# Loading wq, wk and wv four rows to a partition, in an attention and MLP layer on one core

## The chip, the cores and the metric

The kernel runs on one core of one Trainium2 chip. The metric is the device time of one execution in microseconds, as the median of several runs. A run's profile has a span of its own, from the first instruction of the program to the last; the device time is a little longer. The engines are named as the profile names them: PE (TensorE, matrix products; PEld its weight loads), DVE (VectorE), ACT (ScalarE), POOL (GpSimd) and SP (SyncE, which here only issues DMAs).

## The reference

The input x has 2048 rows of 576 values. It is normalised, projected by wq, wk and wv (576 x 576 each), and goes through attention with 32 heads of 18 values in four segments of 512 rows. Each segment attends causally to itself and adds a gated look-up in a memory that the segments before it have built. Then come wo, a residual sum, a second normalisation, and an MLP with 4608 hidden values and gelu.

```
x = A_x
h = x + _A_ref(_layernorm(x, axis=-1), A_wq, A_wk, A_wv, A_wo, A_beta)
h2 = h + _B_ref(_layernorm(h, axis=-1), B_w1, B_b1, B_w2, B_b2)

# in _A_ref, B, S, D, H = 1, 2048, 576, 32
q = (x @ wq)...; k = (x @ wk)...; v = (x @ wv)...        # reshaped to 32 heads, 4 segments
logits = jnp.einsum('bhqd,bhkd->bhqk', qs, ks) * scale + mask
a_dot = jnp.einsum('bhqk,bhkd->bhqd', _softmax(logits, axis=-1), vs)
num = jnp.einsum('bhld,bhde->bhle', pq, M)
den = jnp.einsum('bhld,bhd->bhl', pq, z)[..., None] + 1e-06
o = g * num / den + (1.0 - g) * a_dot
M = M + jnp.einsum('bhld,bhle->bhde', pk, vs)
z = z + jnp.einsum('bhld->bhd', pk)
return o @ wo

# in _B_ref
h = _gelu(jnp.einsum('bsd,df->bsf', x, w1) + b1)
return jnp.einsum('bsf,fd->bsd', h, w2) + b2
```

All inputs are bf16. What matters for this change is the product x @ w over 576 terms: a sum over rows of w, and in whatever order the rows are taken, it is the same sum as long as the values of x are taken in the same order.

## The kernel before

**Tiles.** The 2048 rows are 16 tiles of 128 rows; two tiles make one of 8 chunks of 256 rows. A projection contracts over 576 = 4 x 128 + 64 rows of a weight. So a tile of x, normalised, is turned by PE or by a DMA into `xT`, five blocks of 128 columns; the fifth block holds the last 64 columns of x twice, in its lower and its upper 64 partitions (`again`, lines 398 and 399, writes the second copy). A projection is four matmuls over 128 partitions (`mm4`, line 352) and a tail over 64.

**The tail has two forms.** Whole (`mm_last`, line 356): one matmul over 128 partitions, whose other 64 rows in the weight are zeros (`wpad_q` and the like). Paired (`Part.tail`, line 447): two tails of two column ranges run side by side, one on the lower and one on the upper 64 rows of PE. The set `WHOLE` says which pairs are done as whole tails. `Half.tail` (line 765) is the same for w1.

**The weights of the projections.** `wqkv` has 128 partitions by five blocks by 3 x 576 columns. Block k holds rows 128 k to 128 k + 127, one row to a partition. wq and wk come in two loads each, of 432 and of 144 columns (`wqkv` and `wqkvr`), wv in one; the 64 rows of the tails come in five more. The columns of the projections are cut in parts: 432 of q, 432 of k, 432 of v, and the remaining 144 of each. The first two tiles project the remaining columns of q and k together (288), and those of v alone (144).

**The first normalisation** (`layernorm`). DVE takes the statistics of x, two `BN_STATS` and one `BN_AGGR`. For tiles 0 and 1 it subtracts the mean only (line 381), and the scale, which POOL works out beside it, is multiplied in when the projections leave PSUM (line 519 on ACT, 517 on DVE). For the others ACT (line 394) or DVE (line 387) does both. x of a tile is loaded into one of four buffers, `x_p` and `x_b`.

**The order.** Every piece of work is an `Op` with a number, the engine, and what it reads and writes. Tables of numbers fix the rest: `ORDER` is the sequence in which all are issued, so each engine's own sequence too; `FLIP` lists the ops that run on their second engine (DVE or ACT, DVE or POOL); `PLACE` gives each PSUM result one of eight banks. Every engine works through its own sequence strictly in order, and SP issues all DMAs from one such sequence. At the start PE multiplies zeros 17 times (`zeros`, line 335) while the first tile of x is on its way, and ACT, DVE and POOL fill buffers with zeros.

**Scores and values.** A score group (line 638) is 16 matmuls on 32 rows of PE, four at a time; ACT takes the exponential of 128 x 2048 results (line 642); POOL sets the part above the diagonal to zero (line 646); a value group (line 654) is 16 matmuls, four at a time on 32 columns each. The MLP's matmuls (lines 352 and 872) stand between these. The weights w1 come in pieces of 512 columns through a few buffers, w2 stays in SBUF.

Of the kernel before, what the change touches and what calls it, by code (L numbers as in the profile page):

```python
# [9 lines left out]
ALU = mybir.AluOpType  # L10
# [6 lines left out]
def kernel(  # L17
# [49 lines left out]
    def sbuf(name, shape, dt=BF16):  # L67
        return sb.tile([P] + shape, dt, name=name)

    PLACE = {  # L70
# [35 lines left out]
    }  # L106
    WHOLE = {
        246, 379, 406, 469, 470, 542, 543, 852, 853, 1174, 1175, 1286, 1500, 1501, 2141, 2142,
    }

    class Op:
# [980 lines left out]
```

## Time and profile before

| | |
|---|---|
| Median of 3 runs | 451.72 us (451.48 to 451.95) |
| The profiled execution | 452.2 us, span 450.5 us |
| PE busy | 443.6 us of the span |
| ACT busy | 331.1 us |
| DVE busy | 270.6 us |
| POOL busy | 230.5 us |
| Granted PE clock, mean of the span | 0.999 |

PE is busy nearly throughout, and the granted clock is full. Matmuls overlap in the pipeline, and a matmul's row gives the time from its start to its end, not the time by which it holds up the next; that is read from the starts of neighbouring rows. A row of the timeline has the start, the duration and the count of instructions that stand together; a bracket names what the engine waited for. A row of the waits has the total, the count and the longest.

### The profile page before, as it was taken

To read this page: it belongs to the slowest core of one execution; us is meant where nothing else is said; L and a number is where in the kernel's file an instruction comes from. 1 tells how busy PE (TensorE), PEld (TensorE's weight loads), DVE (VectorE), ACT (ScalarE), POOL (GpSimd) and SP (SyncE) were. 2 spreads that over 40 slices of the span, in tenths; PEclk is the share of its full clock that TensorE was granted. 3 is DMA by queue.
4 is the path that set the end of the run, shared out by engine and by line. 5 is a ranking of instruction groups with operands and counts; after the bars stand their busy time and mean duration, and the time that the engine had idled before them with its cause. 6 is when DMAs were issued, how large, how long until landed. Compare 5 with 4: busy or idle time off the path is not lost.

```text
span 450.5 us, 14512 instructions
## 1 busy us (share of the span) xinstructions
PE 443.6 (98%) x6090; PEld 333.5 (74%) x6090; DVE 270.6 (60%) x620; ACT 331.1 (73%) x313; POOL 230.5 (51%) x416
## 2 busy tenths in 40 slices
PE   7999999999999999999999999999999999999997
PEld 4556977676777777676777677777878888888886
DVE  7899998877797567577648665657352534212111
ACT  8899999998978966979779877687876544241740
POOL 6888956798975387646546865653240203000000
PEclk9999999999999999999999999999999999999999
DMA  7799879979699559796673686586666655474411
GB/s 191 214 205 233 203 192 317 191 140 160 179 197 192 168 134 190 210 166 171 140 175 109 169 183 181 167 209 169 202 180 161 202 169 157 132 224 144 140 41 52
DMA packets 114353, 78.40 MB, mean 174 GB/s; under 512 B 48832, under 2 KB 112240, under 8 KB 114288
## 3 DMA queue, kind: packets, MB, share of 16 engines
q1 hardware_dynamic: 114288, 77.48, 68.5%
q8 instruction: 47, 0.77, 0.8%
q14 instruction: 18, 0.15, 0.1%
HBM read 60.09 MB, written 7.08 MB: 149 GB/s over the span
## 4 chain that ended last, share of the span: by engine, by line
PE 94%; DMA 3%; SPq 2%; DVE 1%; issue 0%; DVEq 0%
PE bank L352 29%; PE bank L872 24%; PE st L352 9%; PE st L872 7%; PE st L638 6%; PE bank L654 5%; PE bank L698 3%; PE bank L765 3%; PE bank L356 2%; DMA w1g<-in_B_w_dram 1%; PE st L698 1%; DMA wqkv<-in_A_wq_dram 1%; PE st L765 1%; PE bank L546 1%; PE bank L608 1%; PE bank L447 1%
## 5 line engine op out<-in xcount | busy, mean ns | idle before, releaser
L642 ACT ACTIVATE pt<-st 128x2048 bf16<-128x2048 f32 x80 | 150.1, 1877 | 39.0 <-PE st L638 31.2
L872 PEld LDWEIGHTS <-hT 128*128 128x128 bf16 x1188 | 110.4, 98 | 28.9 <-issue 1.9
L872 PE MATMUL bank<-w_sb,hT 128*128 128x288 bf16 x900 | 128.9, 286 | 0.0
L352 PEld LDWEIGHTS <-w1g 128*128 128x128 bf16 x944 | 87.6, 98 | 16.3 <-issue 3.8
L646 POOL TENSOR_SCALAR_AFFINE_SELECT pt<-pt 128x512 bf16<-128x512 bf16 x128 | 79.9, 639 | 22.6 <-ACT pt L642 22.0
L352 PE MATMUL bank<-xn2T,w1g 128*128 128x256 bf16 (+1 forms) x728 | 90.8, 268 | 0.0
L786 DVE TENSOR_TENSOR hT<-bank,b1T 128x512 bf16<-128x512 f32 x77 | 51.7, 684 | 42.3 <-PE bank L352 20.8
L807 ACT ACTIVATE hT<-hT 128x1536 bf16<-128x1536 bf16 (+4 forms) x25 | 66.2, 2663 | 7.7 <-DVE hT L786 7.4
L352 PE MATMUL bank<-wqkv,xT 128*128 128x432 bf16 (+1 forms) x216 | 45.5, 342 | 1.1 <-DMA wqkv<-in_A_wq_dram 0.7
L352 PEld LDWEIGHTS <-xT 128*128 128x128 bf16 x264 | 24.6, 98 | 18.1 <-issue 1.4
L603 POOL TENSOR_TENSOR pq<-ek,pq 128x512 bf16<-128x512 bf16 x24 | 27.7, 1154 | 18.9 <-DVE ek L602 14.4
L784 ACT ACTIVATE hT<-bank,b1T 128x256 bf16<-128x256 f32 x54 | 22.1, 471 | 20.1 <-PE bank L765 14.2
L872 PE MATMUL st<-w_sb,hT 128*128 128x288 bf16 (+1 forms) x288 | 35.7, 271 | 0.0
L786 DVE TENSOR_TENSOR hT<-st,b1T 128x512 bf16<-128x512 f32 x24 | 16.4, 687 | 29.9 <-PE st L352 20.2
L784 ACT ACTIVATE hT<-st,b1T 128x256 bf16<-128x256 f32 x32 | 13.3, 474 | 26.2 <-PE st L352 21.3
L638 PE MATMUL st<-QT,KT 32*128 32x128 bf16 x1280 | 32.1, 217 | 0.0
L638 PEld LDWEIGHTS <-KT 32*128 32x128 bf16 x1280 | 18.4, 92 | 15.1 <-issue 11.5
L878 DVE TENSOR_TENSOR ot<-bank,hc 128x288 bf16<-128x288 f32 x25 | 11.2, 447 | 30.6 <-PE bank L872 20.0
L352 PE MATMUL st<-xn2T,w1g 128*128 128x256 bf16 x216 | 29.5, 273 | 0.0
L669 DVE STREAM_TRANSPOSE bank<-bank 128x512 f32<-128x512 f32 x32 | 23.1, 724 | 10.0 <-PE bank L654 9.0
L672 POOL TENSOR_TENSOR r<-r,omg 128x16 f32<-128x16 f32 x32 | 7.2, 226 | 34.9 <-DVE r L670 34.6
L654 PE MATMUL bank<-pt,v_aug 128*19 128x128 bf16 x1280 | 23.8, 220 | 0.0
(162 smaller groups left out, 655.6 us busy)
## 6 DMA issues: line engine op xcount, KB each, us to landing
w1g<-in_B_w_dram SPq DMA_DIRECT2D x57, 512.0 KB, 4.3
w_sb<-in_B_w_dram SPq DMA_DIRECT2D x12, 432.0 KB, 5.5
wqkv<-in_B_w_dram SPq DMA_DIRECT2D x10, 512.0 KB, 3.6
hd<-h_t SPq DMA_DIRECT2D x16, 288.0 KB, 3.5
hc<-hd SPq DMA_DIRECT2D x32, 144.0 KB, 2.7
w1g<-in_B_w_dram SPq DMA_DIRECT2D x114, 32.0 KB, 3.4
x_b<-in_A_x_dram SPq DMA_DIRECT2D x18, 144.0 KB, 3.9
hT<-in_B_w_dram SPq DMA_DIRECT2D x5, 512.0 KB, 4.2
```

The costliest lines, as they stand in the source:

```text
L352: nc.tensor.matmul(out=acc, lhsT=lhsT_of(slice(0, P), k), rhs=rhs_of(slice(0, P), k), start=start and k == 0, stop=False, skip_group_check ...
L603: op(("m_add", n), "POOL", lambda: nc.gpsimd.tensor_tensor(out=pq[:], in0=e_g, in1=pq[:], op=ALU.add), ["ek"], ["pq"])
L638: nc.tensor.matmul(out=st4[:, i, n * P:(n + 1) * P], lhsT=KTs[(2 * s0 + kt) % NK][rows, g, :], rhs=QTs[(2 * c + qt) % NQ][rows, g, :], sta ...
L642: op(("exp", v), "ACT", lambda pt=pt: nc.scalar.activation(out=pt[:], in_=open_four("scores")[:], func=ACT.Exp, scale=scale), [st], [("pt" ...
L646: op(("mask", v), "POOL", lambda n=n, pt=pt: nc.gpsimd.affine_select(out=pt[:, :, n * P:(n + 1) * P], in_=pt[:, :, n * P:(n + 1) * P], pat ...
L654: nc.tensor.matmul(out=bank(ox)[32 * i:32 * i + E, (g % 4) * P:(g % 4) * P + P], lhsT=v_augs[(2 * s0 + kt) % NV][:, G * i + g, :], rhs=pt[ ...
L669: op(("f_T", n), "DVE", lambda: nc.vector.transpose(out=bank(ox), in_=bank(ox)), [], [ox])
L698: nc.tensor.matmul(out=bank(b)[:, 0:HALF], lhsT=xTt[:, k, :], rhs=wo_t[:, k, hs], start=(k == 0), stop=(k == KT - 1))
L784: nc.scalar.activation(out=dst[:, j, :], in_=acc()[:, j, :], func=ACT.Identity, bias=b1T[:, j0 + j:j0 + j + 1], scale=1.0)
L786: return op(name, "DVE", lambda: nc.vector.tensor_tensor(out=dst, in0=acc(), in1=bias, op=ALU.add), [tok, "b1T"], keys, alt=("ACT", by_act ...
L807: op(("gelu", c, f0, f), "ACT", lambda: nc.scalar.activation(out=hT[:, f0:f, :], in_=hT[:, f0:f, :], func=ACT.Gelu_apprx_tanh), [], [("hT" ...
L872: nc.tensor.matmul(out=bank(b)[:, 0:w], lhsT=hT[:, q, tl * P:(tl + 1) * P], rhs=w2_sb[:, q, hs], start=(q == 0), stop=(q == NF - 1))
```

## The change

Partition p now holds rows 4 p to 4 p + 3 of each weight, one behind the other, for the first 512 rows: each partition's part is one run of 4 x 576 values, 4608 bytes, in memory and in SBUF. wq, wk and wv are one load each; the parts of 432 and 144 columns are gone, so a projection now needs the whole of each weight that it reads. The tails keep their five loads. `wqkv` is laid out as three blocks of 4 x 576 and a block of tails behind them.

So that the sums stay the same, block k of the normalised x must hold columns k, k + 4, k + 8 and so on. The normalisation does that as it writes: it reads columns four apart for the first 512. The last 64 columns and their second copy are written by an instruction of its own (`again`), which normalises x twice into 128 columns, on DVE or POOL, where before a copy of 64 columns was made from the normalised tile. It now reads x and its statistics, and no longer waits for the normalisation; the next load of x into the buffer waits for both.

`PLACE`, `FLIP`, `WHOLE` and `ORDER` are new.

```diff
-    wqkv = sbuf("wqkv", [KT, 3 * D])
+    wqkv = sbuf("wqkv", [KT * 3 * D])
+    w_main = wqkv[:, 0:12 * D].rearrange("p (t k n) -> p t k n", t=3, k=4)
+    w_tail = wqkv[:, 12 * D:15 * D].rearrange("p (t n) -> p t n", t=3)
...
     for j, W in enumerate((A_wq, A_wk, A_wv)):
-        for name, lo, hi in (("wqkv", 0, CH), ("wqkvr", CH, D)) if j < 2 else (("wqkv", 0, D),):
-            dma((name, j), hi - lo, 32, lambda j=j, W=W, lo=lo, hi=hi: nc.sync.dma_start(
-                out=wqkv[:, 0:4, j * D + lo:j * D + hi], in_=W[0:512, lo:hi].rearrange("(k p) n -> p k n", p=P)), (), [(name, j)])
+        dma(("wqkv", j), 4 * P * D * 2 / 1024, 8, lambda j=j, W=W: nc.sync.dma_start(
+            out=w_main[:, j], in_=W[0:512, :].rearrange("(p k) n -> p k n", k=4)), (), [("wqkv", j)])
...
+        first = who[0] == "p"
+        parts = [(dst[:, 0:D], src)]
+        if first:
+
+            parts = [(dst[:, 0:512].rearrange("p (k c) -> p k c", k=4), src[:, 0:512].rearrange("p (c k) -> p k c", k=4))]
+            last = (dst[:, 512:XW].rearrange("p (a c) -> p a c", a=2), src[:, 512:D].unsqueeze(1).to_broadcast([P, 2, 64]))
...
+        def normal(engine, o, i):
+            if early:
+                engine.tensor_scalar(out=o, in0=i, scalar1=mv[:, 0:1], scalar2=None, op0=ALU.subtract)
+            else:
+                engine.tensor_scalar(out=o, in0=i, scalar1=mv[:, 0:1], scalar2=rstd[:], op0=ALU.subtract, op1=ALU.mult)
+
         def by_dve():
-            nc.vector.tensor_scalar(out=dst[:, 0:D], in0=src, scalar1=mv[:, 0:1], scalar2=rstd[:], op0=ALU.subtract, op1=ALU.mult)
+            normal(nc.vector, *parts[0])
...
-            op(("apply" + name, t), "ACT", lambda: nc.scalar.activation(out=dst[:, 0:D], in_=src, func=ACT.Identity, bias=nmr[:], scale=rstd[:]),
+            op(("apply" + name, t), "ACT", lambda: nc.scalar.activation(out=parts[0][0], in_=parts[0][1], func=ACT.Identity, bias=nmr[:], scale=rstd[:]),
                [sk, skey], [(*dkey, 0)], alt=("DVE", by_dve))
...
-        op(("again" + name, t), "DVE", lambda: nc.vector.tensor_copy(out=dst[:, D:XW], in_=dst[:, D - 64:D]), [(*dkey, 0)], [(*dkey, 1)],
-           alt=("POOL", lambda: nc.gpsimd.tensor_copy(out=dst[:, D:XW], in_=dst[:, D - 64:D])))
+        if first:
+            op(("again" + name, t), "DVE", lambda: normal(nc.vector, *last), [sk, skey], [(*dkey, 1)], alt=("POOL", lambda: normal(nc.gpsimd, *last)))
...
         def cols(self, r, k):
-            w = wqkv[r, k, :].rearrange("p (t n) -> p t n", t=3)
+            w = w_main[r, :, k, :] if k < 4 else w_tail[r]
...
-        mains = {0: [("wqkv", 0)], 1: [("wqkv", 1)], 2: [("wqkvr", 0), ("wqkvr", 1), ("wqkv", 2)], 3: [("wqkv", 2)],
-                 4: [("wqkvr", 0), ("wqkvr", 1)], 5: [("wqkv", 2)]}[ch]
+        mains = [("wqkv", j) for j in js]
...
     ORDER = [
-        57, 15, 33, 26, 36, 29, 23, 0, 28, 25, 1, 67, 125, 6, 68, 58, 55, 69, 126, 70, 71, 127, 22, 27, 128, 14, 59,
```

SP's sequence at the start, before. The names are the buffer and the input; `wqkv` by 128x4x144 and 128x4x432 are the two parts of wk and wq, 64 rows are a tail:

```order
L265 DMA x_p_76<-in_A_x_dram 128x576
L265 DMA x_p_77<-in_A_x_dram 128x576
L275 DMA wqkv<-in_A_wk_dram 128x4x144
L283 DMA beta_bc<-in_A_beta_dram 128x32
L279 DMA wqkv<-in_A_wq_dram 64x576
L275 DMA wqkv<-in_A_wq_dram 128x4x144
L279 DMA wqkv<-in_A_wk_dram 64x144
L275 DMA wqkv<-in_A_wk_dram 128x4x432
L279 DMA wqkv<-in_A_wk_dram 64x432
L265 DMA x_b_78<-in_A_x_dram 128x576
L275 DMA wqkv<-in_A_wq_dram 128x4x432
L265 DMA x_b_79<-in_A_x_dram 128x576
```

And now:

```order
L268 DMA x_p_76<-in_A_x_dram 128x576
L268 DMA x_p_77<-in_A_x_dram 128x576
L280 DMA wqkv<-in_A_wk_dram 64x432
L268 DMA x_b_78<-in_A_x_dram 128x576
L276 DMA wqkv<-in_A_wk_dram 128x2304
L284 DMA beta_bc<-in_A_beta_dram 128x32
L276 DMA wqkv<-in_A_wq_dram 128x2304
L280 DMA wqkv<-in_A_wq_dram 64x576
L280 DMA wqkv<-in_A_wk_dram 64x144
L292 DMA hT_126<-in_B_b_dram 36x128
L268 DMA x_b_79<-in_A_x_dram 128x576
L276 DMA wqkv<-in_A_wv_dram 128x2304
```

The larger part of wk stood eighth and is now in the fifth load, that of wq stood eleventh and is now in the seventh. Tile 2 of x (`x_b_78`) moved from tenth to fourth.

DVE's sequence from the statistics of tile 0 on, before (`xn1_0` and `xn1_1` are the normalised tiles 0 and 1, `xT0` and `xT1` their transposes):

```order
L367 BN_STATS stats_p0_129<-x_p0_76 128x6 x2
L368 BN_AGGR mv_p0_130<-stats_p0_129 128x2
L381 TENSOR_SCALAR xn1_0_80<-x_p0_76,mv_p0_130 128x576
L261 MEMSET MZacc_74 18x8
L398 COPY xn1_0_80<-xn1_0_80 128x64
L367 BN_STATS stats_p1_133<-x_p1_77 128x6 x2
L368 BN_AGGR mv_p1_134<-stats_p1_133 128x2
L381 TENSOR_SCALAR xn1_1_81<-x_p1_77,mv_p1_134 128x576
L398 COPY xn1_1_81<-xn1_1_81 128x64
L414 COPY xT0_84<-st0_221 128x640
L339 TENSOR_SCALAR g_bc_71<-g_bc_71 128x32
L340 RECIPROCAL g_bc_71<-g_bc_71 128x32
```

And now:

```order
L369 BN_AGGR mv_p0_130<-stats_p0_129 128x2
L392 TENSOR_SCALAR xn1_0_80<-x_p0_76,mv_p0_130 128x128
L392 TENSOR_SCALAR xn1_0_80<-x_p0_76,mv_p0_130 128x512
L264 MEMSET gmz_73 128x8
L368 BN_STATS stats_p1_133<-x_p1_77 128x6 x2
L369 BN_AGGR mv_p1_134<-stats_p1_133 128x2
L392 TENSOR_SCALAR xn1_1_81<-x_p1_77,mv_p1_134 128x512
L264 MEMSET wqkv_62 64x2x72
L264 MEMSET wqkv_62 64x216
L340 TENSOR_SCALAR g_bc_71<-g_bc_71 128x32
L341 RECIPROCAL g_bc_71<-g_bc_71 128x32
L425 COPY xT1_85<-st0_206 128x640
```

The copy of the last 64 columns became a normalisation of 128, ahead of the one of 512; for tile 1 it moved to POOL. The copy of tile 0's transpose left DVE for ACT, and tile 1's came to DVE from there. Both transposes are now written to one PSUM bank, `st0`; before, tile 1's went to another.

More of the change, by code (lines that the diff above doesn't have):

```diff
@@ L213 @@
     W0 = (NCH - 2) * NG
-    done_w = wqkv[:].rearrange("p k n -> p (k n)")
+    done_w = wqkv[:]
     w1_late = [done_w[:, j * W1W:(j + 1) * W1W].rearrange("p (k f) -> p k f", f=512) for j in range(3)]
@@ L279 @@
                 dma(("wqkvt", j, r), (hi - lo) / 8, 4, lambda lo=lo, hi=hi, r=r, j=j, W=W: nc.sync.dma_start(
-                    out=wqkv[r:r + 64, 4, lo:hi], in_=W[512:576, lo - j * D:hi - j * D]), (), [("wqkvt", j, r)])
+                    out=w_tail[r:r + 64, j, lo - j * D:hi - j * D], in_=W[512:576, lo - j * D:hi - j * D]), (), [("wqkvt", j, r)])
     for tl in range(2):
@@ L459, in wkeys_of @@
         tails = [("wqkvt", j, 64 if ch in (1, 3) else 0) for j in js]
-        mains = {0: [("wqkv", 0)], 1: [("wqkv", 1)], 2: [("wqkvr", 0), ("wqkvr", 1), ("wqkv", 2)], 3: [("wqkv", 2)],
-                 4: [("wqkvr", 0), ("wqkvr", 1)], 5: [("wqkv", 2)]}[ch]
+        mains = [("wqkv", j) for j in js]
         return mains + tails + pads
-    WALL = [("wqkv", j) for j in range(3)] + [("wqkvr", j) for j in range(2)] + [("wqkvt", 0, 0)] + [
+    WALL = [("wqkv", j) for j in range(3)] + [("wqkvt", 0, 0)] + [
         ("wqkvt", j, r) for j in (1, 2) for r in (0, 64)] + ["wpad_q", "wpad_k", "wpad_t", "wpad_v"]
```

21 lines of the change are left out of this document (10 added, 11 removed), and 337 rows, old and new, of tables (FLIP, ORDER, PLACE).

## The prediction

> **What bounds the kernel now.** I read the page first, then the waits of PE, then the chain and the timeline of the first 16 us, then the two groups of DMA rows.
>
> ```profile
> PE 443.6 (98%) x6090; PEld 333.5 (74%) x6090; DVE 270.6 (60%) x620; ACT 331.1 (73%) x313; POOL 230.5 (51%) x416
> ...
> PE 94%; DMA 3%; SPq 2%; DVE 1%; issue 0%; DVEq 0%
> ```
> ```profile
> PE bank L335 <- DVE pq L294: 2.4, 1, 2.4
> PE bank L352 <- DMA wqkv<-in_A_wq_dram: 0.7, 1, 0.7
> PE st L765 <- DMA w1g<-in_B_w_dram: 0.5, 1, 0.5
> PE bank L352 <- DMA wqkv<-in_A_wk_dram: 0.2, 1, 0.2
> ```
>
> PE is the bound: 94% of the chain, and after its first instruction all of its listed waits together are 1.4 us. Time can therefore come only from less work on PE, fewer changes between its forms of matmul, or a shorter start. The start is where the loads of wq and wk stand, 0.9 us of those 1.4. Its timeline (start, duration, engine, line; the releaser in brackets), with the two rows of the chain and of the DMA list that belong to it:
>
> ```profile
> 2.73 0.56 SPq L279 DMA_DIRECT2D wqkv<-in_A_wq_dram  x1
> 3.03 0.82 DVE L367 BATCH_NORM_STATS2 stats_p<-x_p 128x6 f32<-128x288 bf16 x2
> 3.31 1.39 ACT L310 COPY hT<-pq 64x256 bf16<-64x256 bf16 x3
> 3.96 0.52 SPq L279 DMA_DIRECT2D wqkv<-in_A_wk_dram  x1
> 4.51 0.59 SPq L275 DMA_DIRECT2D wqkv<-in_A_wk_dram  x1
> 5.57 0.74 PE L411 MATMUL st<-ident,xn 128*128 128x128 bf16 x5
> 5.71 0.58 SPq L265 DMA_DIRECT2D x_b<-in_A_x_dram  x1
> 6.33 0.43 SPq L275 DMA_DIRECT2D wqkv<-in_A_wq_dram  x1
> 7.07 0.69 ACT L415 COPY xT<-bank 128x640 bf16<-128x640 bf16 x1
> 9.24 0.82 DVE L367 BATCH_NORM_STATS2 stats_p<-x_b 128x6 f32<-128x288 bf16 x2 [0.60 <-DMA x_b<-in_A_x_dram]
> ```
> ```profile
> 7.09 0.65 PE L352 MATMUL st<-wqkv,xT 128*128 128x288 bf16 x4
> ...
> 8.80 0.89 PE L352 MATMUL bank<-wqkv,xT 128*128 128x432 bf16 x4 [0.20 <-DMA wqkv<-in_A_wk_dram]
> 9.53 0.35 PE L356 MATMUL bank<-wqkv,xT 128*128 128x432 bf16 x1
> 9.71 0.89 PE L352 MATMUL bank<-wqkv,xT 128*128 128x432 bf16 x4
> ...
> 11.97 0.89 PE L352 MATMUL bank<-wqkv,xT 128*128 128x432 bf16 x4 [0.74 <-DMA wqkv<-in_A_wq_dram]
> ...
> 15.13 0.44 PE L411 MATMUL bank<-ident,xn 128*128 128x128 bf16 x5
> 15.51 0.40 PE L638 MATMUL st<-QT,KT 32*128 32x128 bf16 x16
> 15.84 0.91 PE L352 MATMUL bank<-wqkv,xT 128*128 128x432 bf16 x4
> ```
> ```profile
> 6.33 5.60 DMA wqkv<-in_A_wq_dram
> ```
> ```profile
> wqkv<-in_A_wk_dram SPq DMA_DIRECT2D x1, 432.0 KB, 4.2
> ```
>
> Read them so: x tile 0 is there at 3.03, its first projection starts at 7.09, the projection to k waits for wk at 8.80, the one to q for wq (issued at 6.33, 5.60 us on the way) at 11.97, and the first score stands at 15.51. From 8.80 to 9.53 four matmuls of 432 columns start, so one is 0.18 us; five are 0.90, and five of 288 columns 0.61 at the same rate. From 15.13 to 15.84 lie five transposes (5 x 128 columns, 0.27), 16 score matmuls that run four at a time (0.21), and 0.23 of nothing: a change of form in and one out, 0.12 each.
>
> **The change part by part.**
>
> *Loads.* SP issues about one DMA per 0.5 to 0.6 us, so a place in its order is a time. wk is now fifth (the fifth issue stood at 2.73), wq seventh (3.96), the load of x tile 3 eleventh (6.33). How long a load in pieces of 4608 bytes takes, no row shows. The bounds are the two loads of 432 KB, 4.2 and 5.6 us. I take 4.2 for wk, from the load that was also issued early, with little in front of it, although this one has a third more bytes: wk lands at 6.9. For wq the two rows give 8.2 to 9.6. The rate of the DMA engines by stretch of time (the last two columns are their busy share and GB/s):
>
> ```profile
> 4.00:6.00 2.00, 2.00 (x13) 1.49 (x12) 1.87 (x8) 1.98 (x6) 1.26 (x4) 1.00 0.69 135
> 10.00:12.00 2.00, 1.26 (x14) 0.75 (x12) 1.71 (x7) 1.27 (x3) 1.28 (x4) 1.00 1.04 331
> ```
>
> The low rate stands where the parts of 144 columns, pieces of 288 bytes, were on their way; the high one where pieces of 864 and 1152 bytes were. The Trainium skill (DMA: Bandwidth & Descriptors, Specifications) has 512 bytes as the least transfer for full rate. By that rule the parts of 144 columns gain, and 4608 bytes are no faster than 864: the load of wk would then take 4.2 x 576 / 432 = 5.6 us, and the sum below would be that of the second rival and not mine. The two rows agree with the rule below 512 bytes; above it they say nothing.
>
> *Normalisation of x.* The first 512 columns are now read four apart, and columns 512 to 575 are normalised twice by an instruction of their own in place of a copy:
>
> ```profile
> L381 DVE TENSOR_SCALAR xn<-x_p,mv_p 128x576 bf16<-128x576 bf16 x2 | 0.7, 370 | 0.1
> ...
> L724 DVE TENSOR_SCALAR xn<-h_t,mv_b,rstd_b 128x576 bf16<-128x576 f32 x8 | 4.7, 603 | 1.0 <-POOL rstd_b L719 1.0
> L561 DVE TENSOR_SCALAR ek<-ek 128x576 bf16<-128x576 bf16 x12 | 4.4, 368 | 1.8 <-ACT ek L559 1.8
> L549 DVE COPY QT<-bank 128x1024 bf16<-128x1024 bf16 x6 | 4.1, 676 | 1.3 <-PE bank L546 1.3
> ```
>
> A read four apart has no row. Bounds for 512 columns are 0.33 (the bf16 rate, 370 x 512 / 576) and 0.54 (the slowest row of this operation, 603); I take 0.5. Tile 0 is then ready at 3.03 + 0.82 + 0.2 + 0.2 + 0.5, about 4.8 to 5.0. PE is busy with the eleven multiplications by zero until 5.57, as before, so this costs nothing; without that cover it would cost up to 0.2. In the other 14 tiles, ten of them by ACT, it runs several tiles ahead of PE.
>
> *The start walked through.* The 17 multiplications by zero stay. The copy of tile 0's transpose moves from DVE to ACT, where eight zeroing copies stand ahead of it; three took 1.39 with starts 0.31 apart, all eight some 3.4, so ACT is free by 5.8, before the transpose ends at 6.3, and the copy (0.69) ends at 7.0. Tile 1's transpose now goes to the same bank and waits for that, so the first projection starts at 7.35, not at 7.09. wk (6.9) is there. k of tile 0 runs to 8.25, k of tile 1 to 9.25 (0.1 behind tile 1's copy on DVE), q of tile 0 to 10.15, the 288 columns to 10.75, q of tile 1 to 11.65, without a wait for a load unless wq is at its upper bound (0.3). The transposes of q and k of tile 0 wait for DVE, which evacuates q behind the statistics of x tile 3. That load took 3.5 in the row of x_b above (5.71 to 9.24), so it lands at 9.85, and q is out by 11.85. Two groups of eight transposes (0.43 each), the 288 columns of tile 1, two times 144 columns, five transposes: PE is done with these at about 14.3. The copies that the score needs end on DVE at 11.85 + 1.0 (four small operations) + 0.37 (L561) + 2 x 0.68 (L549) = 14.6. So the first score stands at 14.6 and not at 15.51: 0.9 earlier. Ahead of it 16 transposes fewer have been done (0.85) and ten matmuls of 144 columns more (0.6), 0.25 less work. The start is worth **-0.65 us**; bounds -1.0 and, with the rows' other ends, +0.35.
>
> *Fewer whole tails.* Counted in the two orders, the fifth matmul of a projection over the full 432 columns and 128 rows stands 24 times in place of 32, and pairs of half-row tails 19 times in place of 15. A pair runs side by side:
>
> ```profile
> 184.33 0.36 PE L447 MATMUL st<-wqkv,xT 64*128 64x432 bf16 x2
> 184.52 0.34 PE L447 MATMUL bank<-wqkv,xT 64*128 64x432 bf16 x2
> 184.70 0.27 PE L765 MATMUL st<-xn2T,w1g 64*128 64x256 bf16 x1
> 185.44 0.39 PE L765 MATMUL st<-xn2T,w1g 64*128 64x256 bf16 x3 [0.47 <-DMA w1g<-in_B_w_dram]
> ```
>
> Two pairs from 184.33 to 184.70, 0.18 each. So -8 x 0.18 + 4 x 0.18 = **-0.72**. All other matmuls have the same count and columns.
>
> *Changes of form.* Between full, half-row, score and value matmuls the order before changes 257 times, the new one 262 times: 5 x 0.12 = **+0.60**.
>
> *Stalls behind the start.* The one of before is in the last two rows: 0.47 us for a load of a w1 tail. It may go, and another may come; the new order has as many loads and moves them all. I take **0**, bounds -0.5 (none) and +2.
>
> Sum: -0.65 - 0.72 + 0.60 = -0.77. The profiled execution took 452.2 (span 450.5, 1.7 around it), 0.5 above the median of 451.72; nothing changes around the span. From the median: 450.95, and I say **450.9**. About 0.2% (0.9 us) is what a measurement of this kernel can tell from no change.
>
> **The rivals.**
>
> *No stall at all:* the new order loses the 0.47 and brings none. For it: PE's waits are down to that one; against: its loads pass the same single queue. 450.9 - 0.5 = 450.4.
>
> *Long pieces are no faster:* wk takes 5.6 us, lands at 8.3, and the first projection starts 1.0 later. The start is then worth -0.65 + 1.0 = +0.35, and the time is 451.72 + 0.35 - 0.72 + 0.60 = 451.95. For it: the second 432 KB load took just that. Against: that load had five others beside it. This is what the rule on 512 bytes in the Trainium skill (DMA: Bandwidth & Descriptors, Specifications) would make of it.
>
> *SP's queue held up by GpSimd, slower:* a buffer of x was free when its normalisation had read it; now the instruction for the last 64 columns reads it too, in 13 of 16 tiles on GpSimd. The next load of x waits for that in SP's queue, and the loads of w1 stand behind it.
>
> ```profile
> SPq L265 <- DVE xn L387: 4.7, 2, 3.8
> ...
> 179.46 0.47 SPq L744 DMA_DIRECT2D w1g<-in_B_w_dram  x1
> ```
> ```profile
> L706 POOL TENSOR_TENSOR h_t<-h_t,b_bc 128x576 f32<-128x576 f32 x16 | 20.5, 1279 | 1.9 <-DVE xn L724 1.2 <-ACT xn L729 0.6
> ```
>
> SP waits at such loads already, once for 3.8 us. The w1 tail issued at 179.46, 5.2 us before its use at 184.70, was late by 0.47, so w1 has nothing to spare there, and each further delay counts in full. Two operations of the size of L706 ahead on GpSimd are 2.5 us: 450.9 + 2.5 = 453.4. It decides from about 1.7 us on, where it has eaten the 0.77 and 0.9 more. Against: GpSimd is busy half of the span, and the order lets x be loaded a chunk ahead.
>
> **How the numbers follow.** My case has a chance of 0.48 and a spread of some 0.8 us about 450.9, as the unknown stalls and the walk make it: just over half of it is faster by more than 0.2%, the rest within. No stall at all: 0.16, faster. Long pieces no faster: 0.13, nearly all within 0.2%. SP held up: 0.23, nearly all slower. That makes 0.42 faster, 0.36 within, 0.22 slower. The range reaches from 449.7 (no stall, and the start at its better bound) to 453.2, which leaves out the worst of SP's case and a little below: under 2 in 10. My own case alone is 450.1 to 451.7.
>
> **What the profile of the changed kernel would show.** Right: no wait of PE for wqkv; the first projection near 7.35 and the first score near 14.6; 24 whole fifth matmuls and 38 tails of 432 columns; the loads of wk and wq landing by 6.9 and 9.6; the normalisation near 0.5 us on DVE. Wrong: a wait for wk or wq in PE's list (long pieces), DVE waiting for x tile 3 until after 11, waits of SP at the loads of x for GpSimd with waits of PE for w1g of 0.5 us or more behind them, or a sum of PE's waits after its first instruction above 2 us.

## The result, and the profile after

The changed kernel takes 453.44 us (median of 11 runs, 452.30 to 454.48), the kernel before 451.95 beside it (11 runs, 451.11 to 452.54). The ratio is 1.0034, with a 95% interval of 1.0022 to 1.0046: slower by about 1.5 us, where 0.8 us faster was forecast, and just above the range. The profiled execution took 453.44, its span is 451.7 (before: 452.2 and 450.5).

The page after: busy times, and the chain that ended last.

```profile
PE 444.1 (98%) x6090; PEld 332.7 (74%) x6090; DVE 274.0 (61%) x623; ACT 329.3 (73%) x311; POOL 236.9 (52%) x416
...
PE 91%; POOL 3%; DMA 2%; DVE 1%; ACT 1%; SPq 1%; issue 0%; POOLq 0%
```

The waits of PE after (for what, us in total, times, longest):

```profile
PE bank L336 <- DVE pq L295: 2.5, 1, 2.5
PE st L353 <- DVE xT L425: 1.3, 1, 1.3
PE bank L353 <- DMA xT<-xn: 0.4, 1, 0.4
PE bank L664 <- issue: 0.2, 1, 0.2
PE bank L353 <- DMA wqkv<-in_A_wk_dram: 0.2, 1, 0.2
```

The wait for wq and the one for a w1 tail are gone. In their place stands one of 1.3 us for a copy on DVE, and two small ones near 36 and 53. The chain of the changed kernel, in its first 17 us, tells who made the copy late:

```profile
3.41 5.26 DMA beta_bc<-in_A_beta_dram
...
8.70 0.24 ACT g_bc L339
...
8.96 0.19 DVE g_bc L340
...
9.17 0.35 DVE g_bc L341
9.53 0.36 DVE xT L425
...
9.93 0.58 PE st L353 x3
```

And its timeline (start, duration, engine, line; the releaser in brackets):

```profile
3.41 0.43 SPq L284 DMA_DIRECT2D beta_bc<-in_A_beta_dram  x1
3.89 0.43 SPq L276 DMA_DIRECT2D wqkv<-in_A_wq_dram  x1
...
7.53 0.89 PE L353 MATMUL bank<-wqkv,xT 128*128 128x432 bf16 x4 [0.18 <-DMA wqkv<-in_A_wk_dram]
...
8.70 0.23 ACT L339 ACTIVATE g_bc<-beta_bc 128x32 f32<-128x32 bf16 x1 [1.84 <-DMA beta_bc<-in_A_beta_dram]
...
9.44 0.43 DVE L425 COPY xT<-st 128x640 bf16<-128x640 bf16 x1
...
9.93 0.90 PE L353 MATMUL st<-wqkv,xT 128*128 128x432 bf16 x4 [1.33 <-DVE xT L425]
...
11.55 0.82 DVE L368 BATCH_NORM_STATS2 stats_p<-x_b 128x6 f32<-128x288 bf16 x2 [0.27 <-DMA x_b<-in_A_x_dram]
...
16.02 0.40 PE L648 MATMUL st<-QT,KT 32*128 32x128 bf16 x16
```

The load of beta, 8 KB for the gate, is issued right behind wk and is on its way for 5.3 us (before: 2.7). ACT waits 1.84 for it with the exponential, DVE waits for ACT with the addition and the reciprocal of the gate, and the copy of tile 1's transposed x stands behind those two on DVE. So k of tile 1 starts at 9.93 and the first score at 16.02, 0.51 after the 15.51 of before. With the 0.25 us less work ahead of it, the start cost 0.76 where it was to bring 0.65. The last matmul starts 1.3 later than before (448.69 and 447.38), so 0.55 came behind the start.

Each profile is one execution. Three pairs of the kernels below have the same loads and instructions up to the first score, and it stood at 16.02 and 15.90, at 14.94 and 15.65, and at 15.42 and 14.64 in them. So a start that is read from one profile is uncertain by up to 0.8 us. With beta's load behind wk and ahead of wq, four kernels with the new rows and order have it at 15.9 to 16.4; with this load third, on a queue of its own or left out, five have it at 14.6 to 15.7.

### The profile page after: what moved, and what is told of

Same layout as the page of the kernel before. It is cut to its first block, busy times and chain, and to the rows that moved or that the text cites. A ratio compares the mean times of both kernels' runs of the same rounds, so it can differ in the third digit from the quotient of the medians.

```text
span 451.7 us, 14511 instructions
## 1 busy us (share of the span) xinstructions
PE 444.1 (98%) x6090; PEld 332.7 (74%) x6090; DVE 274.0 (61%) x623; ACT 329.3 (73%) x311; POOL 236.9 (52%) x416
## 4 chain that ended last, share of the span: by engine, by line
PE 91%; POOL 3%; DMA 2%; DVE 1%; ACT 1%; SPq 1%; issue 0%; POOLq 0%
PE bank L353 27%; PE bank L882 25%; PE st L353 10%; PE st L882 6%; PE st L648 5%; PE bank L664 5%; PE bank L708 3%; PE bank L775 3%; POOL pt L656 1%; PE st L775 1%; DMA beta_bc<-in_A_beta_dram 1%; PE bank L357 1%; PE bank L618 1%; DMA xT<-xn 1%; PE st L708 1%; PE bank L458 1%
## 5 line engine op out<-in xcount | busy, mean ns | idle before, releaser
L882 PE MATMUL bank<-w_sb,hT 128*128 128x288 bf16 (+1 forms) x936 | 131.2, 284 | 0.0
L353 PEld LDWEIGHTS <-w1g 128*128 128x128 bf16 x944 | 87.5, 98 | 16.4 <-issue 3.4
L353 PE MATMUL bank<-xn2T,w1g 128*128 128x256 bf16 (+1 forms) x696 | 86.2, 268 | 0.0
L796 DVE TENSOR_TENSOR hT<-bank,b1T 128x512 bf16<-128x512 f32 x75 | 50.7, 684 | 47.9 <-PE bank L353 35.8
L353 PE MATMUL bank<-wqkv,xT 128*128 128x432 bf16 (+2 forms) x212 | 43.7, 341 | 0.6 <-DMA xT<-xn 0.4
L353 PEld LDWEIGHTS <-xT 128*128 128x128 bf16 x264 | 23.6, 98 | 20.3 <-issue 1.9
L882 PE MATMUL st<-w_sb,hT 128*128 128x288 bf16 (+1 forms) x252 | 33.6, 277 | 0.0
L353 PE MATMUL st<-xn2T,w1g 128*128 128x256 bf16 x248 | 33.6, 273 | 0.0
L794 ACT ACTIVATE hT<-bank,b1T 128x256 bf16<-128x256 f32 x56 | 23.2, 473 | 13.4 <-PE bank L353 9.5
L888 DVE TENSOR_TENSOR ot<-bank,hc 128x288 bf16<-128x288 f32 (+1 forms) x26 | 11.6, 447 | 32.0 <-PE bank L882 30.7
L664 PEld LDWEIGHTS <-v_aug 128*19 128x19 bf16 x1280 | 18.2, 91 | 6.4 <-issue 3.7
```

The source lines that it names most:

```text
L353: nc.tensor.matmul(out=acc, lhsT=lhsT_of(slice(0, P), k), rhs=rhs_of(slice(0, P), k), start=start and k == 0, stop=False, skip_group_check ...
L664: nc.tensor.matmul(out=bank(ox)[32 * i:32 * i + E, (g % 4) * P:(g % 4) * P + P], lhsT=v_augs[(2 * s0 + kt) % NV][:, G * i + g, :], rhs=pt[ ...
L794: nc.scalar.activation(out=dst[:, j, :], in_=acc()[:, j, :], func=ACT.Identity, bias=b1T[:, j0 + j:j0 + j + 1], scale=1.0)
L796: return op(name, "DVE", lambda: nc.vector.tensor_tensor(out=dst, in0=acc(), in1=bias, op=ALU.add), [tok, "b1T"], keys, alt=("ACT", by_act ...
L882: nc.tensor.matmul(out=bank(b)[:, 0:w], lhsT=hT[:, q, tl * P:(tl + 1) * P], rhs=w2_sb[:, q, hs], start=(q == 0), stop=(q == NF - 1))
```

## Experiments

Each ratio is to the kernel before, in runs on the same chip, with its 95% interval. One thousandth is 0.45 us. The difference of two such ratios is uncertain by about 0.0017, or 0.8 us, where both intervals are as wide as that of the changed kernel (the two half-widths added as squares).

**The copy ahead of the gate.** Only DVE's order is changed:

```diff
 DVE:
-  g_add, g_rec,
   copy of tile 1's xT,
+  g_add, g_rec,
   statistics of x tile 2
```

> The changed kernel with two small operations on DVE, the addition and the reciprocal of the gate (g_add, g_rec), moved behind the copy of tile 1's transposed x; no load moves. Theory A, the start was lost because these two wait for the exponential of beta, whose load lands at 8.7, and the copy of tile 1 stands behind them: the copy starts near 7.4 in place of 9.44, k of tile 1 at 8.45 in place of 9.93, and the time falls by most of that 1.3 us, to 452.1 to 452.7. Rival B, the next thing in the start takes the stall over (the evacuation of q of tile 0 stands on DVE behind the statistics of x tile 3, whose load lands at 11.5): the first score moves from 16.02 to no better than 15.4, PE waits at the transposes of q instead, and the time falls by 0.6 at most, 452.8 to 453.4.

Measured: 452.88, ratio 1.0025 (1.0015 to 1.0036). Its waits of PE:

```profile
PE bank L353 <- DMA wqkv<-in_A_wq_dram: 1.8, 1, 1.8
PE bank L353 <- DMA xT<-xn: 0.5, 1, 0.5
```

k of tile 1 started at 8.37, and then PE stood for wq until 11.24: 7.3 us from issue to use. The first score stood at 16.41, not earlier than in the changed kernel, and the two ratios are too close to be told apart. B was right that something takes the stall over, but wrong on what: a load was late beneath it, in a place where the forecast had 8.2 to 9.6.

**beta third in SP's queue.**

```diff
 SP: x_p 0, x_p 1,
+    beta,
     wk tail, x_p 2, wk,
-    beta,
     wq, ...
```

> The changed kernel with the load of beta moved from sixth to third place in SP's queue, ahead of the long loads; nothing else. If its 5.3 us on the way are the company of the long pieces, it now lands in 2.7, near 4.5, g_add and g_rec are done before tile 1 is transposed, k of tile 1 starts near 8.8 (the load of wk is issued 0.4 later and lands near 7.9), and the time falls by about 0.9, to 452.5. If 5.3 us is what this load takes in any place, it lands near 7.0, the copy of tile 1 is ready at 8.3, and the gain is nearly the same, 0.6 to 0.9; the landing time tells them apart.

Measured: 452.53, ratio 1.0012 (1.0000 to 1.0025). beta took 2.6 us, so 5.3 is its place and not its nature; q of tile 0 started at 9.77 and the first score at 14.94. wq, issued at 3.87 as before this edit, was there 1.5 us sooner than in the first experiment (0.8 sooner, at 10.48, in a later kernel with the same start). So beta does not only come late behind wk: it also holds up wq. As this edit moves nothing but that load, the difference from the changed kernel, 0.0022 in the ratio or 1.0 us, uncertain by 0.8, is the price of its place.

**Shorter pieces.** One line gives the tile the old arrangement of columns, so that a piece is 1152 bytes:

```diff
-    w_main = wqkv[:, 0:12 * D].rearrange("p (t k n) -> p t k n", t=3, k=4)
+    w_main = wqkv[:, 0:12 * D].rearrange("p (k t n) -> p t k n", t=3, k=4)
```

> The changed kernel with the three weights side by side in each row of the tile again, so that the same loads, in the same order and with the same four rows for each partition, go in pieces of 1152 bytes in place of 4608; nothing else. If the long pieces load faster, wk (4.6 us from issue to use in the changed kernel) and wq land later, by up to 1 us, and the time rises to 453.6 to 454.4. If they only stand in the way of the small loads behind them, beta lands 2 us earlier (2.7 on the way in place of 5.3), the wait of 1.3 us is gone, and the time falls to 452.4. If the length of a piece does not matter above 512 bytes, everything lands as it did and the time stays within 0.3 of 453.4.

Measured: 453.39, ratio 1.0036 (1.0022 to 1.0050). Between pieces of 1152 and of 4608 bytes these runs tell no difference. Each of these loads stood 0.14 to 0.16 us longer on SP, and beta came as late as before (ACT had it at 8.49).

**beta left out, in both kernels.** The tile is filled with zeros by GpSimd:

```diff
-    dma("beta", 8, 8, lambda: nc.sync.dma_start(out=beta_bc[:], in_=A_beta.partition_broadcast(P)), (), ["beta"])
+    op("beta", "POOL", lambda: nc.gpsimd.memset(beta_bc[:], 0.0), (), ["beta"])
```

> The changed kernel without the load of beta: the tile is filled with zeros by GpSimd, so the gate is computed from zeros and not from the input. This prices that load by itself. If it is what the start lacks (theory C), PE has no wait for the copy of tile 1 and little for wq, which lands near 9.5, the first score stands near 14.8, and the time is 452.0 to 452.3. If bytes alone set the landing of wq, PE waits 1.5 to 1.8 us for it as in the first experiment, and the time is 452.8 to 453.0.

> The kernel before the change without the load of beta (zeros by GpSimd, so the gate is not computed from the input): the price of that load there. If the price is much below the 1.6 us that it has in the changed kernel (453.44 against 451.81), the new place of beta in the queue is what the start lost: 451.3 or more. If it is the same, 450.1, beta was a cost in both.

Measured: the changed kernel 451.81, ratio 1.0006 (0.9996 to 1.0016); the kernel before 451.07, ratio 0.9987 (0.9978 to 0.9995). So this load costs the changed kernel 1.3 us by the ratios (1.6 by the medians) and the kernel before 0.6 (0.7). By this, beta's new place lost the difference, 0.7 to 0.9 us; with three intervals in it, this is uncertain by 0.8, so these two runs alone don't show it. The kernel before came out between its two cases, nearer to the 451.3 by which the place matters. The DMA engines by microsecond (the last two columns are their busy share and GB/s), from 6 to 8, in the changed kernel and then in the one without beta:

```profile
6.00:7.00 1.00, 0.88 (x11) 0.64 (x9) 0.81 (x3) 0.77 (x2) 0.90 (x2) 1.00 0.51 82
7.00:8.00 1.00, 0.82 (x8) 0.51 (x8) 0.10 (x1) 0.00 (x0) 0.92 (x5) 1.00 0.66 229
```
```profile
6.00:7.00 1.00, 0.90 (x10) 0.67 (x9) 0.81 (x3) 0.79 (x3) 0.91 (x2) 1.00 0.99 387
7.00:8.00 1.00, 0.97 (x9) 0.64 (x9) 0.93 (x5) 0.99 (x4) 0.92 (x5) 1.00 1.01 386
```

From 6 to 7 the rate falls to 82 GB/s in the one and stays at 387 in the other, although wq waits to be moved in both. Counted in the trace, some 106 packets of 64 bytes (of beta's 128) and 26 pieces of 4608 start from 6.0 to 7.5 in the changed kernel; without beta it is 128 pieces. The Trainium skill (DMA: Bandwidth & Descriptors, Queues, rings and completion order) says that each DMA engine takes the descriptors of one ring in order. The trace agrees as far as it goes: wq's pieces stood behind beta's. Why 64 bytes from one place take so long, it doesn't show.

**beta on a queue of its own.** ACT issues the load as its first instruction:

```diff
-    dma("beta", 8, 8, lambda: nc.sync.dma_start(...), (), ["beta"])
+    op("beta", "ACT", lambda: nc.scalar.dma_start(...), (), ["beta"])
```

> The changed kernel with the load of beta issued by ACT as its first instruction, on a queue of its own, and no longer by SP; nothing else is moved. If what the change lost at the start is the place of these 128 small packets ahead of wq in SP's queue, taking them out of it is worth as much as leaving the load away (451.81): wq lands near 9.5, the first score stands near 14.7, the time is 451.6 to 452.1. If the packets hold up the DMA engines from whatever queue they come, it stays above 452.5.

> The kernel before the change with the load of beta issued by ACT first, out of SP's queue; nothing else. There beta stood fourth, with only small loads behind it, and was on its way for 2.7 us. If its place was harmless there, the time stays within 0.3 of before. If it costs the kernel before as much as the changed one, this is faster by 1 us or more, and beta does not explain the difference between the two.

Measured: the changed kernel 452.19, ratio 1.0006 (0.9996 to 1.0016), the ratio that it has without beta; the kernel before 451.25, ratio 0.9997 (0.9987 to 1.0007), no difference that can be told. The first score of the changed kernel stood at 15.42 in this profile, where 14.7 was expected, and PE stood 0.9 us near 52 (below). This edit takes beta out of the ring, brings it 2.6 us forward and spares SP one issue; it doesn't separate the three. The small packets slow the DMA engines from this queue too: from 2 to 3 us the rate was 119 to 162 GB/s in the three kernels with beta on ACT's queue, and 266 and 271 in the two without beta. But that was before the first piece of wk started (4.2 in the changed kernel with this edit).

**beta late.** In three kernels beta goes behind wq and x tile 3, and the gate's operations on ACT and DVE move down, each time to another place. The second and the third also have the two later edits that are told below (w2, tile 5's transpose).

```diff
 SP: x_p 0, x_p 1, wk tail, x_p 2, wk,
-    beta,
     wq, wq tail, wk tail, b1, x_p 3,
+    beta,
     wv, ...
 ACT (first):           g_exp directly ahead of the evacuation of k of tile 0
 ACT (second, third):   g_exp behind the evacuations of q and k of both tiles
 DVE (first, second):   the gate's operations in one row behind it
 DVE (third):           two at a time, between evacuations
```

> The changed kernel with the load of beta moved behind the loads of wq and of x tile 3 in SP's queue, and the exponential on ACT and the small gate operations on DVE moved down to where their results are first needed; nothing else. Theory C, formed from the DMA packets: beta goes out as 128 packets of 64 bytes, and while these trickle (5.5 to 8.5 us in the changed kernel, a rate of 50 to 110 GB/s) the pieces of wq behind them in the same queue wait; wq is what the start then lacks. By it wq lands near 9.5 to 9.8 in place of 11.2, the first score stands near 15.0 in place of 16.0, and the time falls by 0.9 to 1.4, to 452.0 to 452.5. Rival, the sheer bytes of wk, wq and x set the start and beta has no part in it: wq lands at 11 as in the first experiment, PE waits 1.8 for it, and the time is that of the first experiment, 452.9.

Measured: 453.18, ratio 1.0028 (1.0015 to 1.0041). wq came early enough that PE did not wait for it, as theory C says, and the time did not follow: the first score stood at 16.55, where 15.0 was expected. The exponential, in order on ACT ahead of the evacuation of k, now held ACT for 2.6 us, and PE waited 0.7 for ACT. PE also waited 0.7 for wk, which took 5.3 us; in six kernels with the same loads ahead of it, wk took 3.8 to 5.3.

> The kernel of the combined experiment (452.59) with the exponential of beta on ACT behind the evacuations of q and k of both tiles, so that ACT does not stand 1.7 to 2.6 us for beta ahead of them, and the gate operations on DVE behind that. If the waits for ACT at 12.2 and 12.7 (0.38 each in that profile) were all that moving beta back had brought, they are gone and the time is 451.8. If the load of x tile 3 or of wk then sets the start, it stays within 0.3 of 452.6.

Measured: 452.95, ratio 1.0027 (1.0018 to 1.0037), just above both cases. The first score stood earlier than in any other kernel, and DVE took that back; its rows, and those of PE:

```profile
14.17 0.18 DVE L340 TENSOR_SCALAR g_bc<-g_bc 128x32 f32<-128x32 f32 x1
14.39 0.35 DVE L341 RECIPROCAL g_bc<-g_bc 128x32 f32<-128x32 f32 x1
14.78 1.09 DVE L343 TENSOR_SCALAR omg<-g_bc 32x8 f32<-32x8 f32 x4
...
16.04 0.35 DVE L527 TENSOR_SCALAR v_aug<-bank,rs_early 128x144 bf16<-128x144 f32 x1
```
```profile
14.32 0.40 PE L648 MATMUL st<-QT,KT 32*128 32x128 bf16 x16
...
16.44 0.61 PE L556 MATMUL bank<-ident,qk_pad 128*128 128x128 bf16 x8 [0.69 <-DVE v_aug L527]
17.46 0.34 PE L353 MATMUL bank<-wqkv,xT 128*128 128x432 bf16 x1 [0.42 <-DVE v_aug L527]
```

The gate's small operations are 1.9 us of DVE in one row here, and the evacuation of v came behind them.

> The experiment before (beta behind wq and x tile 3, its exponential behind the first evacuations on ACT, w2 and tile 5's transpose moved) with the nine small gate operations on DVE no longer in one row: two each behind the evacuations of v of tile 1, its transposed q, the last evacuation of tile 0 and the statistics of x tile 5. In that experiment the first score stood at 14.32, 1.7 before the changed kernel's, and then PE stood 0.9 and 0.6 at 15.4 and 16.8 behind DVE's row of gate operations. If that row took the gain back, both waits go and the time is 451.0 to 451.6, at or under the kernel before. If DVE is full there whatever stands in it, the waits come a little later and the time stays at 452.5 or more.

Measured: 451.92, ratio 1.0007 (0.9990 to 1.0023). That is between the two cases, and 0.0020 under the experiment before, just more than the two intervals leave uncertain. Waits came later, at 22 and 24 us (0.6 and 0.7 for DVE).

**The rows and the order apart.** The new rows with the old order, and the old rows with the new order:

> The rows and loads of the changed kernel (four rows for each partition, no column parts, the same normalisation) with the order, the banks, the engines and the whole tails of the kernel before; the whole loads of wk and wq stand where the parts of 144 columns stood, and the second normalisation of the last 64 columns is moved ahead of the next load of x in five tiles. If the new order is what costs, the time is that of before or less, 451.0 to 452.2. If the new form of the rows costs by itself (the slower normalisation, the loads of x that wait for GpSimd, the long loads), it is 452.5 to 454.

> The old rows of the weights, in their old loads with column parts, and the old normalisation (one operation and a copy of 64 columns), with the new order, banks, engines and whole tails; each load of 144 columns stands right behind the one of 432 that it was split from, and the copy stands behind its normalisation in seven tiles. If the new rows cost by themselves (GpSimd normalises 128 columns in 0.8 us where it copied 64 in 0.24, and x is held longer), this is faster than the changed kernel, 452.0 to 452.8. If the two further loads in front of wq, and the pieces of 288 bytes, cost more than that, it is slower, 453.8 to 455.

```diff
 new rows:  loads whole, 4 rows to a partition, `again` reads x
-  new ORDER, PLACE, FLIP, WHOLE
+  those of before (whole loads where the 144-column parts stood)

 old rows:  loads of 432 and 144 columns, `again` copies xn
-  ORDER, PLACE, FLIP, WHOLE of before
+  the new ones (each 144-column load behind its 432)
```

Measured: 463.39, ratio 1.0258 (1.0235 to 1.0281), and 454.51, ratio 1.0059 (1.0044 to 1.0075). Both cross pairs are slower than both kernels, so neither rows nor order can be priced alone; the first is far outside both of its cases. Of the second, the case of the slower loads came true in its time; its waits of PE are spread over the first 55 us, and what they come from was not told apart. In the first, SP's waits at the loads of x (line 268) and the timeline near 139 show the third rival of the prediction at work:

```profile
SPq L268 <- POOL xn L394: 13.0, 3, 8.2
```
```profile
134.92 0.81 POOL L394 TENSOR_SCALAR xn<-x_p,mv_p,rstd_p 128x128 bf16<-128x128 bf16 x1
135.75 0.35 SPq L268 DMA_DIRECT2D x_p<-in_A_x_dram  x1
...
138.78 0.46 DVE L368 BATCH_NORM_STATS2 stats_p<-x_p 128x6 f32<-128x288 bf16 x1 [4.88 <-DMA x_p<-in_A_x_dram]
...
139.89 0.88 PE L882 MATMUL bank<-w_sb,hT 128*128 128x288 bf16 x3 [3.99 <-DVE hT L796]
```

The load of x waits for GpSimd's part of the normalisation, DVE waits for the load, and PE 4.0 us for DVE. The new order keeps clear of this: SP's list has no such wait.

The first pair lost more than these waits. Its page has the granted PE clock in tenths, by 40 slices of the span (9 is 90% or more):

```profile
PEclk9999999999997999999999999999999999999999
```

The slice marked 7 stands right behind the stop of 4.0 us: from 140 to 146 the granted clock was 0.50 to 0.53. It was also 0.73 from 10 to 15, behind a wait of 2.1 us for wv. The mean is 0.989 in this profile and 1.00 in that of the changed kernel, and 0.011 of the span is 5 us. So up to some 5 of the 11.6 us are the lower clock, an estimate from these figures; the five runs had means of 0.985 to 0.996. What lowered it isn't shown.

**The stall near 53.** Two loads of w2 are issued later, and nothing else:

```diff
 SP:
-   w2 5,
    hd 0,
-   w2 2,
    x_p 8, Tk 4, Tx 6, six loads of w1,
+   w2 5, w2 2,
```

> The changed kernel with two loads of w2 (432 KB each, used from 85 us on), which it issues at 44.5 and 46.7 us, moved to about 60 us; nothing else. PE stands still near 53 for 0.3 to 1.1 us in the four kernels with this order, between two value matmuls whose operands are all there. Theory D, it waits for its own code: a packet of 16 KB of instructions starts at 51.2, at the moment at which the DMA engines, full since 46, come free. By it the packet comes some microseconds earlier and the stall is gone: minus 0.4 in the profile, up to minus 0.9 in the median, 452.6 to 453.0. Rival, the stall is in the order (an operand whose wait the profile doesn't show): it stays at 0.3 to 1.1 and the time at 453.4.

Measured: 452.72, ratio 1.0018 (1.0006 to 1.0030), and the stall near 53 is gone; the time is not clearly less than that of the changed kernel, and the profile has a new wait of 0.9 us for DVE near 30. The changed kernel near 53 ("issue" is a wait for nothing that the profile shows); its DMA queue for instructions from 51.2 to 53.4 (packets, MB, share of the engines); and the same place with this edit:

```profile
52.78 0.45 PE L664 MATMUL bank<-pt,v_aug 128*19 128x128 bf16 x18
...
53.43 0.40 PE L664 MATMUL bank<-pt,v_aug 128*19 128x128 bf16 x14 [0.20 <-issue]
```
```profile
q8 instruction: 1, 0.02, 2.8%
```
```profile
52.88 0.63 PE L664 MATMUL bank<-pt,v_aug 128*19 128x128 bf16 x32
```

Worked out from the packets and the starts in the traces: in the eight kernels of this study that have the stall near 53 (0.3 to 1.1 us), it ends 1.2 to 1.4 us after the end of a packet of 16 KB of instructions; in the six with this order that have none, that packet had ended 1.2 us or more before PE came to the place. In two of these six, both with the two loads of w2 later, and in one of the eight, PE stood 0.5 to 0.8 us near 46 or 48 instead or as well, among matmuls of 128 columns. These stalls too ended 1.3 to 1.5 us after a packet of 16 KB, the one before. The rows of the two in PE's list of waits (beta third with the later edits, and beta late with the gate's operations spread out):

```profile
PE bank L353 <- issue: 0.3, 1, 0.3
PE bank L353 <- issue: 0.6, 1, 0.6
```

So PE waits for its code; this is argued from the times of eleven stalls, as no row names the packet as what ended the wait. With the edit the packet started 0.7 earlier (50.53, not 51.23). That the loads had delayed it is likely, not shown: with other edits added (below), PE was earlier at the place and the stall was there again, although the two loads were away. The Trainium skill (Runtime: NRT & Kernel Launch, Instruction fetch mechanics) has instructions fetched in blocks of 16 KiB, mostly hidden. The size agrees with the trace; here it was not hidden.

**The three places together.** The two loads of w2 later, the transposing load of tile 5 ahead of two loads of w1 tails, and beta late, third, or on ACT's queue:

```diff
 SP:
+   Tx 5,
    w1 tail, w1 tail,
-   Tx 5,
```

> The two edits before this (beta late with the gate operations, the two loads of w2 later) together, and the transposing load of tile 5's x moved ahead of two loads of w1 tails, so that it goes out at 31.3 in place of 32.3; PE waited 0.6 for it at 36.0. If the three places are what the change lost, they add: minus 1.1, minus 0.5, minus 0.5 from 453.4, so 451.3, just under the kernel before. If the stalls only move on, it is 452.0 or more.

> The second experiment's edit (beta third in SP's queue, ahead of wk) together with the two loads of w2 later and the transposing load of tile 5's x one millisecond-free step earlier, that is ahead of two loads of w1 tails. If the three places carry what the change lost, they add to the 452.53 that beta first alone took: the stall for code near 52 (0.9 in that profile) gone or halved, the wait for tile 5's transpose gone: 451.4 to 451.9, at or just under the kernel before. If the stalls only move on, it stays at 452.5.

> The kernel of the experiment before this one, with the two loads of w2 later and tile 5's transposing load ahead of two loads of w1 tails. If the start and the two stalls near 36 and 53 add, as they did from 452.53 to 451.66 with beta third, the time is 450.7 to 451.2, under the kernel before. If they only move on, 451.6 or more.

Measured: 452.59, ratio 1.0017 (1.0003 to 1.0031); 451.66, 0.9998 (0.9988 to 1.0009); 451.59, 0.9995 (0.9985 to 1.0004). In the first, moving beta back cost PE two gaps of 0.38 behind ACT, and the stall near 53 was there again (0.6). The other two take back all that the change lost and are level with the kernel before; the gain that the last one's sum promised beyond that did not come. In the profile of the last, PE's only wait of note is the first one:

```profile
PE bank L336 <- DVE pq L295: 2.5, 1, 2.5
```

No version was shown to beat the kernel before.

## Why the prediction was wrong, point by point

*The start, -0.65: the step that failed.* The walk has k of tile 1 start "0.1 behind tile 1's copy on DVE". It left out what DVE does ahead of that copy: two operations of the gate (lines 340 and 341), which wait for ACT, which waits for the load of beta. The order shows the two; the walk never asked when beta lands, now that it is sixth and behind wk. The start measured +0.76, so 1.4 of the 2.3 us between forecast (-0.8) and result (+1.5), as far as one profile of each kernel tells. The late beta acted twice, on the copy and on wq: with the copy moved ahead the start gained nothing, with the load itself moved or left out it did.

*wq at 8.2 to 9.6: wrong too, and hidden by that.* With the copy out of the way, PE stood for wq until 11.24 (in the changed kernel's own profile wq was in use at 10.85). I carried a latency over from another place in the queue and didn't ask what is in front of it in small pieces. wk landed near 7.5, not 6.9, and x tile 3 near 11.5, not 9.85. The row of wk in the DMA list after (KB, us to landing):

```profile
wqkv<-in_A_wk_dram SPq DMA_DIRECT2D x1, 576.0 KB, 4.5
```

*The rest of the walk: right in two executions.* Without beta, and with beta on ACT's queue and the later edits, the first score stood where the forecast had it, at 14.6. The first of these executions was the fastest of its 11 runs. With beta on ACT's queue and no later edit, where the start is the same, it stood at 15.42. Without beta:

```profile
14.64 0.40 PE L648 MATMUL st<-QT,KT 32*128 32x128 bf16 x16
```

*Whole tails, -0.72: right.* Of 432 columns there are 20 + 4 = 24 left, and 38 half-row tails. At the rates that the prediction reads, the columns of all matmuls behind the first score take 0.47 less than before, which is the 0.25 from ahead of it and the -0.72. The rows (count, least, median and longest ns, first and last start, forms):

```profile
L357 PE MATMUL bank<-wqkv,xT x23: 226/346/346, 8.3 to 260.1; 128*128 128x432 bf16 x20, 128*128 128x144 bf16 x2, 128*128 128x288 bf16 x1
...
L357 PE MATMUL st<-wqkv,xT x5: 286/346/346, 10.7 to 278.0; 128*128 128x432 bf16 x4, 128*128 128x288 bf16 x1
```
```profile
L458 PE MATMUL bank<-wqkv,xT x30: 342/353/353, 21.2 to 251.2; 64*128 64x432 bf16 x30
L458 PE MATMUL st<-wqkv,xT x8: 342/342/353, 138.1 to 208.4; 64*128 64x432 bf16 x8
```

*Changes of form, +0.60: fits, not tested by itself.* The trace has 262 against 257. By the distance of starts, a change takes about 0.10 beyond the columns of the matmul in front of it. Behind the first score, the gaps at changes of form and between half-row matmuls, without stalls, come to some 0.6 more than before.

*Stalls behind the start, 0: mis-sized.* The one at 184.7 went, as far as hoped. Gaps of over 0.25 us, from start to start and without the columns of the matmul in front, are 0.30, 0.58 and 0.41 (at 32, 36 and 53) where before had 0.27, 0.29 and 0.69 (at 24, 35 and 185). Their sums are level, 1.29 and 1.25. But the stretch behind the start came to +0.55 and not to -0.12. The missing 0.6 or so lies in smaller gaps: five of 0.07 to 0.21, at 17.7, 24.8, 27.2, 47.4 and 69.1, between full matmuls or between value matmuls, where the kernel before has none over 0.05. What PE waited for in them wasn't traced.

This loss stays when the start is mended. With beta on ACT's queue in both, and the later edits in the new one, the two kernels are level, 0.9995 and 0.9997. In the profiles the new one has its first score 0.75 us earlier (14.64, and 15.39 before), and its last matmul starts at the same time (446.29 and 446.26). So a better start was had and was lost again behind it.

*Normalisation, 0.5 on DVE, hidden: right there, no price on GpSimd.* The groups of the changed kernel by line, with their shapes (busy, mean ns of one):

```profile
L394 POOL TENSOR_SCALAR xn<-x_p,mv_p,rstd_p 128x128 bf16<-128x128 bf16 x10 | 8.2, 819 | 0.0
...
L744 POOL COPY xn<-xn 128x64 bf16<-128x64 bf16 x9 | 2.2, 245 | 10.3 <-DVE xn L734 10.3
...
L394 DVE TENSOR_SCALAR xn<-x_p,mv_p,rstd_p 128x512 bf16<-128x512 bf16 x4 | 2.1, 532 | 0.0
...
L392 DVE TENSOR_SCALAR xn<-x_p,mv_p 128x512 bf16<-128x512 bf16 x2 | 1.0, 484 | 0.0
```

Reading four apart, 512 columns take DVE 0.48 to 0.53; in the kernel before, 576 columns in a row took 0.37 (the mean subtracted) and 0.53 (both operations). The last 64 columns, twice, take GpSimd 0.82, where a copy like the one in line 744 takes 0.24; the prediction gave that no price. No wait of PE was shown to come from it in the new order. In tile 5 PE waited 0.4 for the transposing load behind this operation, but the operation ended at 31.3 and the load went out at 32.27, behind two loads of w1 tails in SP's queue.

*The rivals.* "Long pieces no faster" was right in its premise (1152 and 4608 bytes gave 453.39 and 453.44) and wrong in its path: wk took 4.5 us (3.8 to 5.3 in six kernels), not 5.6. "SP held up by GpSimd" hit the time, 453.4, by chance: in the new order SP waits at the loads of x without PE waiting behind it. "No stall" did not come. The rival that was missing is a small load in front of a large one.

## What to carry to other kernels

A load that is small in bytes is not small in a queue: give each load of the start a landing time, and before moving a large one, look at what stands in front of it and which engine waits, in order, for the small one. When such a wait is taken away, look under it before counting the gain; here another load was late beneath the first, and in three further edits the wait moved to ACT, to DVE and to later tiles. Two profiles of one start can differ by 0.8 us, so a start is compared by several kernels or by the time of many runs. An order belongs to the loads and instructions that it was made for: old rows in the new order and new rows in the old one were both slower than either kernel.

## What was not expected of the hardware

A broadcast of 64 bytes to 128 partitions brought the DMA engines of the core from 387 to 82 GB/s for about a microsecond while a load of 576 KB was queued behind it. And PE, busy for 98% of the span, stood for up to 1.1 us in a stretch of short matmuls, by all signs for its own instructions. Where PE had stood for 4.0 us, its granted clock was 0.50 to 0.53 for the six microseconds behind.
